# Moving the q/k transposes to the front of the SyncE queue and two v projections ahead of the last q and k, in a fused attention and gated-MLP kernel

## The chip, the cores and the metric

The kernel runs on one core of one Trainium2 chip. The metric is the device time of one execution in microseconds (us); lower is better. The core has five engines with instruction streams of their own: TensorE (PE, matrix products), ScalarE (ACT), VectorE (DVE), GpSimd (POOL) and SyncE (SP). SP here does nothing but issue DMA transfers, in the order in which they are written. Matrix products land in PSUM, which the program treats as eight banks of 512 fp32 columns; ACT and DVE empty the banks into on-chip memory.

## What is computed

The input `x` is 2048 rows of 576 columns, bf16. After a layer norm, two branches read it, and their product is added to `x`:

```python
def _A_ref(x, wqkv, wo):
    H = 32; Dh = D // H; W = 256                       # Dh = 18
    q, k, v = ...                                      # x @ wqkv, split in heads
    scores = einsum("bhqd,bhkd->bhqk", q, k) * Dh ** -0.5
    # causal, and only the last 256 keys
    p = softmax(where(mask, scores, -1e9))
    return einsum("bhqk,bhkd->bhqd", p, v) @ wo

def _B_ref(x, w_gate, w_up, w_down):                   # F = 4608
    return (sigmoid(x @ w_gate) * (x @ w_up)) @ w_down

xn = layernorm(A_x)
out = A_x + _A_ref(xn, ...) * silu(_B_ref(xn, ...))
```

## The kernel before

**Chunks and stages.** The rows are worked through in four chunks of 512 (`NCH`), each made of four blocks of 128 rows. For one chunk the stages on PE are: the q, k and v projections (line 521, twelve of them: q, k and v of each block), the gate and up products of the MLP (line 898), in which the attention scores (line 688) and the products with v (line 745) are mixed in, and the down projection `f2` (line 1045), which is made for two blocks at a time: first pair (blocks 0 and 1), second pair (blocks 2 and 3). The output projection `wo` (line 815) and the next chunk's twelve q/k/v projections stand between the first and the second pair. This change of chunks, which occurs three times, is the place that this study is about. In PE's order it reads: first pair of f2, `wo` of blocks 0 and 2, six projections, `wo` of blocks 1 and 3, six projections, second pair of f2, gate and up products of the next chunk.

**The path of q and k.** A projection writes a pair of PSUM banks. For q a DVE instruction, for k an ACT instruction (both line 579) empties it into a slot of the ring `pk`. A DMA transpose (`qkt`, line 603) then brings the slot into `qkp`, with channels on the partitions. The ring has three slots, taken in the order q0, k0, q1, k1, q2, k2, q3, k3: so k1 can be emptied only when the transpose of q0 has landed, q2 after that of k0, k2 after q1, q3 after k1, k3 after q2. A v projection (line 617) is emptied by two ACT and two DVE instructions (line 625) straight into its place `vau`; it waits for no transpose. From the keys in `qkp`, DVE makes masked copies `kd` (line 672) for each group of four heads, which the scores read.

**Banks.** f2's second pair needs the pairs of banks (0,1) and (2,3) (`F2B`). `QKV_BANKS` says in which banks the last projections may go.

**The other transfers in this place.** `wx` (`load_x`, line 847) loads two small pieces of the gate and up weights (32 KB each, tile `sat`), the first of which (gate) the gate/up stage of the next chunk uses in two early steps, whose place `XP` sets; the second (up) is used at the end of that stage. `out` (`final_cols`, line 1141) stores a finished block of 128 rows from the ring `xf`, of two slots, and `xf` (`load_xf`) loads the rows of x for a later block into the same ring: the loads for blocks 2 and 3 need the slots of blocks 0 and 1, and so wait for those stores to have landed. The twelve weight pieces of the next chunk's first three gate/up groups (`load9`, tile `wgs`, line 405) wait for the first steps of f2's second pair (`W_GATE`).

**How the order is made.** The program lists operations with dependences and plans them with a list scheduler (`schedule`, line 1145), which writes one fixed instruction order per engine; the chip then runs each engine's list in order and waits by semaphores. `deps` become waits on the chip; `odeps` only order the plan. Among the operations that an engine could take, the scheduler takes the one with the smallest start plus 40 ns times `prio` (`PRIO_NS`). A DMA counts as done in the plan at its landing, and what is ordered behind it becomes free a slack later:

```python
                free[e] = st + o.occ
                bs = max(free[e] + DMA_LAT_NS, bw)
                bw = bs + o.nbytes / DMA_BYTES_PER_NS
                o.done = bw
...
                elif o.lane is not None:
                    t = o.done + o.slack
```

These constants decide an order; they are not measured times.

Of the kernel before, what the change touches and what calls it, by code (L numbers as in the profile page):

```python
# [59 lines left out]
AVOID_NS = 20000.0  # L60
RBN = 4
XS = (13, 1, 1, 1)
XP = (4, 0)
RUN = 3
WX_PRIO = -1
WX_FT = 7
WD_AT = (14, 18, 22, 28, 29, 30, 31, 32, 33)
QKV_FIRST = "q0 q1 v0 v1 q2 v2 k0 v3 k1 q3 k2 k3"
QKV_NEXT = "q0 k0 q1 v0 v1 k1 q2 k2 v2 q3 k3 v3"
QKV_GATE = 2  # L70
QKV_PRIO = -2
QKV_CHAIN = 1
QKV_WO = {"v1": (0,), "q2": (1,)}
WO_QKV = {"k0": (1,)}
QKV_BANKS = {"q3": ((0, 1), (2, 3)), "k3": ((4, 5), (6, 7)), "v3": ((4, 5), (6, 7))}
QKV_F2 = (1, 8)
LAST = 448
W_GATE = 2
# [138 lines left out]
class Builder:  # L217
# [98 lines left out]
    def build(self):  # L316
        self.r_xr = Ring(NXR)
        self.r_xnr = Ring(NXNR)
        self.r_xn = Ring(1)
        self.r_w = Ring(RW)  # L320
        self.r_t = Ring(RT)
        self.r_pk = Ring(RPK)
        self.r_exp = Ring(NEXP)
        self.r_s = Ring(RS)
        self.r_xf = Ring(RXF)
        self.r_kd = Ring(RKD)
        self.r_rec = Ring(RREC)
        self.r_bn = Ring(RBN)
        self.op_f1 = {}
        self.build_init()  # L330
        self.op_pv = [[None] * NHG for _ in range(NCH)]
        self.op_sc = [[[] for _ in range(NHG)] for _ in range(NCH)]
        self.op_on = [[None] * NHG for _ in range(NCH)]
        self.op_mul = [[None] * NHG for _ in range(NCH)]
        self.all_kd = {}
        self.op_oc = [[[], []] for _ in range(NCH)]
        self.op_v = [None] * NQB
        self.op_tail = [None] * NHG
        self.op_hT = {}
        self.f2_last = None  # L340
        for c in range(NCH):
            self.build_ln(c)
            if c == 0:
                self.build_weights()
                self.build_wd()
            self.build_qkv(c)
            self.last_mul = None
            self.build_attn(c)
            self.load_x(c)
            self.op_pkz = [self.op("POOL", 2000, lambda e: e.memset(self.pk[:, 1:RPK, :, :], 0.0), f"pkz:{c}",  # L350
                                   deps=self.op_on[c], prio=1)]
            if c == 0:
                self.op_wo = []
            self.build_wo(c)
            self.build_ffn(c)
            if c == 0:
                self.build_late_weights()
                for o in self.ops:
                    if o.name in ("wo:0:00", "wo:0:10"):
                        o.add_dep(self.op_wo)  # L360
                for k, o in enumerate(self.op_wo):
                    self.f2_ops[(1, k % 5)].add_dep(o)
# [178 lines left out]
            "p t (h d) -> p t h d", d=DH)  # L541

    def build_qkv(self, c):
        self.op_q, self.op_k, self.op_qkt, self.op_qe = [], [], [], []
        old = [o for l in self.op_sc[c - 1] for o in l] + self.op_tail if c > 0 else []
        order = QKV_FIRST if c == 0 else QKV_NEXT
        prev = None
        for w in order.split():
            i, j = int(w[1]), "qkv".index(w[0])
            o = (self.build_v if j == 2 else self.build_qk)(c, i, j, old)  # L550
            if c > 0:
                o.odeps += [self.op_wop[x] for x in QKV_WO.get(w, ())]
                o.odeps += ([prev] if prev and QKV_CHAIN else []) + (self.op_xn[QKV_GATE] if not prev else []) + ([self.f2_ops[QKV_F2]] if QKV_F2 else [])
                o.prio = QKV_PRIO
                for x in WO_QKV.get(w, ()):
                    self.op_wof[x].odeps.append(o)
                for ps in o.alloc:
                    ps.cands = QKV_BANKS.get(w, ps.cands)
            prev = o

    def build_qk(self, c, i, j, old):
        if c == 0:
            both = self.pk[:, 0:2, :, :].rearrange("p j h d -> p (j h d)") if i == 0 else \
                self.expr[:, 2 * i - 2:2 * i, :, :].rearrange("p a b c -> p (a b c)")
            pk = both.rearrange("p (g q r s d) -> p q s g r d", g=NHG, q=2, r=2, s=2)[:, j, :, :, :, 0:DH]
            dpk = []
        else:
            spk, dpk = self.r_pk.take()
            full = self.pk[:, spk, :, :]
            pk = full[:, :, 0:DH].rearrange("p (h s) d -> p s h d", s=2)  # L570
        o, ps = self.project(c, i, j, f"qk:{c}:{i}:{j}", [], self.op_pv[c - 1][NHG - 1] if c > 0 else None)

        deps = [o, self.op_pkz] + dpk + (self.op_ez[i - 1:i] if c == 0 and i > 0 else []) + (self.op_on[c - 1] if c > 0 else [])

        def f_ev(e, part, act):
            src, dst = self.halves(ps)[:, part], pk[:, part]
            if c == 0:
                dst, src = dst[:, 0], src[:, 0].rearrange("p (g r) d -> p g r d", r=2)
            return e.activation(dst, src, ACTF.Copy) if act else e.tensor_copy(dst, src)  # L579
        ev = []  # L580
        for k, (part, act) in enumerate(((slice(0, 1), 1), (slice(1, 2), 0)) if c == 0 else ((slice(0, 2), j),)):
            n = D // 2 if c == 0 else D
            ev.append(self.rd("ACT" if act else "DVE", act_ns(n) if act else dve_ns(n),
                              lambda e, part=part, act=act: f_ev(e, part, act), f"qke:{c}:{i}:{j}:{k}", deps=deps, prio=1,
                              psum=[ps]))
        if c == 0:
            if j == 0:
                self.op_qe.append(ev)
                return o
            dst = self.qkp[:, :, :].rearrange("p g (j c) -> p (g j) c", j=2)[:, :, i * P:(i + 1) * P]  # L590
            dm = self.dma(dst, both, 2 * XT0_BYTES * 8 * P * P * 2, f"qkt:{c}:{i}", ("qk", i), deps=ev + self.op_qe[i] + old,
                          prio=0, issue=XT0_ISSUE_NS, transpose=True, slack=XT0_SLACK)
            if i > 0:
                for k in (2 * i - 2, 2 * i - 1):
                    self.r_exp.release(k, dm)
            else:
                for k in (0, 1):
                    self.r_pk.rel[k].append(dm)
            self.op_q.append(dm)
            self.op_k.append(dm)  # L600
        else:
            c0 = j * KO + i * P
            dm = self.dma(self.qkp[:, :, c0:c0 + P], full.rearrange("p h d -> p (h d)"), XT_BYTES * 8 * P * P * 2,
                          f"qkt:{c}:{i}:{j}", ("qk", i, j), deps=ev + old, prio=0, issue=XT_ISSUE_NS, transpose=True)
            self.r_pk.release(spk, dm)
            (self.op_q, self.op_k)[j].append(dm)
        self.op_qkt.append(dm)
        return o
# [47 lines left out]
    def build_kd(self, c, hg):  # L656
        self.slots_kd, self.ops_kd = {}, {}
        for g in range(1 if c == 0 else 0, 3):
# [4 lines left out]
            for half in range(2):  # L663
                def f_kd(e, g=g, s_=s_, half=half):
                    if g == 0:
                        src = self.qkp[:, hg, :].rearrange("p (j c) -> p j c", j=2)[:, :, CH:CH + P].rearrange(
                            "p j (b c) -> p j b c", b=2)
                        dst = self.kd[:, s_, :, half, :].rearrange("p (j b) c -> p j b c", j=2)
                    else:
                        src = self.qkp[:, hg, KO + (g - 1) * 256:KO + g * 256].rearrange("p (b c) -> p b c", b=4)  # L670
                        dst = self.kd[:, s_, :, half, :]
                    return e.tensor_scalar(dst, src, self.hm[:, half:half + 1], None, ALU.mult)  # L672
                self.ops_kd[g].append(self.op("DVE", KD_NS, f_kd, f"kd:{c}:{hg}:{g}{half}", deps=deps, prio=KD_PRIO))
        self.all_kd[hg] = [o for l in self.ops_kd.values() for o in l]

    def build_unit(self, c, hg, u, pieces, masks):
# [170 lines left out]
    def load_x(self, c):  # L847
# [4 lines left out]
        for n, (w, f, j, r0) in enumerate(src):  # L852
            a = w[:, f:f + P].rearrange("(j p) c -> p j c", p=64)[:, j:j + 3:2, :]
            dst = self.sat[r0:r0 + 64, self.sx, 0:2 * P].rearrange("p (j c) -> p j c", j=2)
            self.op_wx.append(self.dma(dst, a, 2 * W_FACTOR * 64 * 2 * P * 2, f"wx{n}:{c}", ("wx", n), deps=dx, prio=WX_PRIO))
            self.r_s.release(self.sx, self.op_wx[-1])

    def build_ffn(self, c):
# [257 lines left out]
    def build_final(self, sb, ps, o_f2, sth, dth, ss, o_s):  # L1116
# [2 lines left out]
        self.r_s.release(ss, q2)  # L1119
        self.r_exp.release(sth, q3)  # L1120
        self.r_xf.release(sx, o_o)

    def final_cols(self, sb, ps, o_f2, sth, dth, ss, o_s, sx, o_x, c0, c1):
        op = self.op
# [285 lines left out]
```

## Time and profile before

| | |
|---|---|
| median of three runs | 559.36 us (559.29, 559.36, 560.3) |
| the profiled execution | 559.26 us, of which the profile's span is 557.5 us and 1.76 us lies around it |
| PE busy | 552.2 us, 99% of the span; granted clock 1.00 |
| DVE, ACT, POOL busy | 312.2, 279.4, 29.2 us |
| DMA | 73.35 MB, mean 132 GB/s |
| the three changes of chunks (first projection to the first f2 step of the second pair) | from 122.27, 259.56 and 397.69 us to 137.71, 275.83 and 413.13 us |

In the lines of the profile a row reads: start, duration, engine, source line, operation, output <- input, shapes, count; a bracket at the end is the engine's idle time just before and what ended it. SPq is SP's issuing of a DMA; "to landing" is the time from the issue to the data's arrival.

### The profile page before, as it was taken

To read this page: it belongs to the slowest core of one execution; us is meant where nothing else is said; L and a number is where in the kernel's file an instruction comes from. 1 tells how busy PE (TensorE), PEld (TensorE's weight loads), DVE (VectorE), ACT (ScalarE), POOL (GpSimd) and SP (SyncE) were. 2 spreads that over 40 slices of the span, in tenths; PEclk is the share of its full clock that TensorE was granted. 3 is DMA by queue.
4 is the path that set the end of the run, shared out by engine and by line. 5 is a ranking of instruction groups with operands and counts; after the bars stand their busy time and mean duration, and the time that the engine had idled before them with its cause. 6 is when DMAs were issued, how large, how long until landed. Compare 5 with 4: busy or idle time off the path is not lost.

```text
span 557.5 us, 18764 instructions
## 1 busy us (share of the span) xinstructions
PE 552.2 (99%) x8144; PEld 310.2 (56%) x8146; DVE 312.2 (56%) x906; ACT 279.4 (50%) x395; POOL 29.2 (5%) x58
## 2 busy tenths in 40 slices
PE   8999999999999999999999999999999999999998
PEld 5755555567555455556655554545665554554554
DVE  5436998425067988633407798843430785885111
ACT  7436886124076767602307778740330875873031
POOL 3000110100000100010000011001000000000100
PEclk9999999999999999999999999999999999999999
DMA  8999868938945666235993666422399355651001
GB/s 201 221 203 209 210 183 215 241 62 152 205 106 132 141 155 138 56 52 66 167 214 89 150 142 148 104 63 65 63 169 203 86 130 130 139 130 34 21 25 41
DMA packets 125929, 73.35 MB, mean 132 GB/s; under 512 B 54680, under 2 KB 125336, under 8 KB 125848
## 3 DMA queue, kind: packets, MB, share of 16 engines
q1 hardware_dynamic: 125848, 72.16, 61.5%
q8 instruction: 64, 1.05, 0.8%
q14 instruction: 17, 0.14, 0.1%
HBM read 55.48 MB, written 2.36 MB: 104 GB/s over the span
## 4 chain that ended last, share of the span: by engine, by line
PE 96%; DMA 2%; ACT 1%; DVE 1%; issue 0%; ACTq 0%; SPq 0%
PE ps L898 50%; PE ps L1045 22%; PE ps L521 7%; PE ps L688 6%; PE ps L745 4%; PE ps L815 3%; DMA qkp<-pk 2%; PE ps L1100 2%; PE ps L1076 2%; PE ps L396 1%; ACT xn L507 0%; DVE pk L579 0%; DVE expr L1135 0%; ACT expr L1133 0%; ACT sat L840 0%
## 5 line engine op out<-in xcount | busy, mean ns | idle before, releaser
L898 PE MATMUL ps<-xn,wgs 64*128 64x512 bf16 x2522 | 299.3, 376 | 0.0
L898 PEld LDWEIGHTS ps<-xn,wgs 64*128 64x128 bf16 x2522 | 121.5, 94 | 114.1 <-issue 1.4
L703 ACT ACTIVATE expr<-ps 128x1024 bf16<-128x1024 f32 (+1 forms) x152 | 150.7, 1019 | 23.9 <-PE ps L688 23.8
L916 DVE SCALAR_TENSOR_TENSOR hT<-tring,ps 128x512 bf16<-128x512 bf16 x144 | 98.2, 682 | 54.8 <-PE ps L898 35.0
L912 ACT ACTIVATE tring<-ps 128x512 bf16<-128x512 f32 x144 | 86.4, 600 | 82.3 <-PE ps L898 61.8
L1045 PE MATMUL ps<-wd_sb,hT 64*128 64x512 bf16 (+1 forms) x2016 | 125.5, 283 | 0.7 <-DVE pk L579 0.7
L1045 PEld LDWEIGHTS ps<-wd_sb,hT 64*128 64x128 bf16 x2016 | 65.8, 94 | 59.4 <-issue 1.0
L717 DVE TENSOR_TENSOR expr<-expr,m 128x256 bf16<-128x256 bf16 (+1 forms) x272 | 61.3, 267 | 6.4 <-ACT expr L703 5.9
L688 PE MATMUL ps<-qkp,kd 64*128 64x320 bf16 (+4 forms) x720 | 56.7, 252 | 0.0
L521 PE MATMUL ps<-wqkv_sb,xn 64*128 64x288 bf16 x864 | 54.4, 283 | 0.1
L688 PEld LDWEIGHTS ps<-qkp,kd 64*128 64x128 bf16 x720 | 34.2, 94 | 33.3 <-issue 0.8
L672 DVE TENSOR_SCALAR kd<-qkp,hm 128x256 bf16<-128x256 bf16 x176 | 40.5, 290 | 16.6 <-DMA qkp<-pk 14.3
L1133 ACT ACTIVATE expr<-ps 128x576 bf16<-128x576 f32 (+2 forms) x17 | 9.8, 620 | 76.8 <-PE ps L1045 61.4
L521 PEld LDWEIGHTS ps<-wqkv_sb,xn 64*128 64x128 bf16 x864 | 43.0, 94 | 9.4 <-ACT xn L507 0.2
L1135 DVE SCALAR_TENSOR_TENSOR expr<-expr,ps 128x576 bf16<-128x576 bf16 x12 | 8.5, 751 | 63.8 <-ACT expr L1133 63.8
L840 ACT ACTIVATE sat<-ps 128x576 bf16<-128x576 f32 x16 | 9.5, 648 | 64.8 <-PE ps L815 64.8
L1137 DVE TENSOR_TENSOR expr<-expr,sat 128x576 bf16<-128x576 bf16 (+2 forms) x17 | 7.2, 437 | 43.7 <-ACT expr L1133 34.4
L761 DVE STREAM_TRANSPOSE pk<-ps 128x512 f32<-128x512 f32 x32 | 21.4, 697 | 17.2 <-PE ps L745 17.2
L727 POOL COPY qkp<-qkp 128x256 bf16<-128x256 bf16 x24 | 10.2, 425 | 264.4 <-DVE kd L672 264.4
L778 DVE STREAM_TRANSPOSE op__63<-pk 128x512 bf16<-128x512 bf16 x32 | 22.3, 701 | 0.1
L745 PEld LDWEIGHTS ps<-expr,vau 64*32 64x32 bf16 x1440 | 18.1, 92 | 7.4 <-issue 5.5
L745 PE MATMUL ps<-expr,vau 64*32 64x320 bf16 (+4 forms) x1440 | 20.8, 254 | 0.0
(55 smaller groups left out, 223.0 us busy)
## 6 DMA issues: line engine op xcount, KB each, us to landing
wgs<-in_B_w_gate_dram SPq DMA_DIRECT2D x47, 240.0 KB, 3.8
wgs<-in_B_w_up_dram SPq DMA_DIRECT2D x47, 240.0 KB, 4.8
wgs<-in_B_w_up_dram SPq DMA_DIRECT2D x47, 192.0 KB, 4.2
wgs<-in_B_w_gate_dram SPq DMA_DIRECT2D x47, 192.0 KB, 4.6
wd_sb<-in_B_w_down_dram SPq DMA_DIRECT2D x9, 576.0 KB, 6.9
xf<-in_A_x_dram SPq DMA_DIRECT2D x18, 144.0 KB, 2.5
out_dram<-xf SPq DMA_DIRECT2D x15, 144.0 KB, 2.1
xr<-in_A_x_dram SPq DMA_DIRECT2D x14, 144.0 KB, 4.2
```

The lines of the kernel that those rows point to most:

```text
L521: r = e.matmul(self.bank(ps, HV, hf), self.xn[r0:r0 + 64, k, i * P:(i + 1) * P], self.wqkv_sb[r0:r0 + 64, j, k, :], start=(k == 0), stop=( ...
L672: return e.tensor_scalar(dst, src, self.hm[:, half:half + 1], None, ALU.mult)
L688: i = e.matmul(self.bank(ps, 512, r)[:, pos * 64:(pos + n) * 64], w, self.qkp[r0:r0 + 64, hg, q0 * 64:(q0 + n) * 64], start=True, stop=Tru ...
L703: return e.activation(self.expr[:, es, :, 0:ncol], src, ACTF.Exp, scale=SM_SCALE)
L717: return e.tensor_tensor(ap, ap, m, ALU.mult)
L745: r = e.matmul(self.bank(ps2[s_])[32 * cg:32 * cg + 32, q0 * 64:(q0 + n) * 64], vf[:, v0:v0 + 32], self.expr[p0:p0 + 64, es, cg % 2, pos * ...
L761: tr = self.rd("DVE", dve_ns(CH), lambda e, tf=tf, s_=s_: e.transpose(tf, self.bank(ps2[s_])), f"t1:{c}:{t}", deps=[o, self.op_mul[c][t - ...
L778: t2 = self.op("DVE", dve_ns(CH), lambda e, on=on: e.transpose(self.op_[:, hg % NOT, :], on.rearrange("p g d -> p (g d)")), f"t2:{c}:{hg}" ...
L898: return e.matmul(self.bank((pg, pu)[gu][ft]), w, self.xn[r0:r0 + 64, i, :], start=first, stop=last, tile_position=(r0, 0))
L912: return e.activation(self.tring[:, st_, :], self.bank(ps), ACTF.Tanh, scale=0.5)
L916: return e.scalar_tensor_tensor(self.hT[:, ft, :], self.tring[:, st_, :], 1.0, self.bank(ps), ALU.add, ALU.mult)
L1045: r = e.matmul(self.ps[:, b + n0:b + n1], self.hT[r0:r0 + 64, ft, i * P:(i + 1) * P], self.wd_sb[r0:r0 + 64, q, ft % WDG, n0:n1], start=(s ...
```

## The change

Six edits, all of them on the chunks after the first except the first one, which holds for every chunk:

1. `XP`: the two steps that use the small gate piece stand at step 5 and 6 of the stretch, not 4 and 5.
2. The q/k transposes get the priority -4 (was 0) in the plan of SP.
3. The stores of blocks 0 and 1 of the chunk before, and both small weight pieces, are ordered behind all eight transposes, with priority -3 (`odeps`, so the plan only; no wait is added on the chip).
4. The order of the projections ends "v2 v3 q3 k3" (was "v2 q3 k3 v3").
5. `QKV_BANKS`: v2 and v3 go into banks (0,1) or (2,3), q3 and k3 into (4,5) or (6,7) (before: q3 in the first two, k3 and v3 in the others, v2 free).
6. The first head group's `kd` copies are ordered behind the emptying of every q and k and of the last v.

```diff
-XP = (4, 0)
+XP = (5, 0)
+HELD_PRIO = -3
+QKT_PRIO = -4
-QKV_NEXT = "q0 k0 q1 v0 v1 k1 q2 k2 v2 q3 k3 v3"
+QKV_NEXT = "q0 k0 q1 v0 v1 k1 q2 k2 v2 v3 q3 k3"
-QKV_BANKS = {"q3": ((0, 1), (2, 3)), "k3": ((4, 5), (6, 7)), "v3": ((4, 5), (6, 7))}
+QKV_BANKS = {"v2": ((0, 1), (2, 3)), "v3": ((0, 1), (2, 3)), "q3": ((4, 5), (6, 7)), "k3": ((4, 5), (6, 7))}
...
     def build_qkv(self, c):
...
             prev = o
+        for o in self.op_out[-QPC:-FIN]:
+            o.odeps += self.op_qkt
+            o.prio = HELD_PRIO
+        self.op_out = []
...
+        self.op_ev += ev
...
-                          f"qkt:{c}:{i}:{j}", ("qk", i, j), deps=ev + old, prio=0, issue=XT_ISSUE_NS, transpose=True)
+                          f"qkt:{c}:{i}:{j}", ("qk", i, j), deps=ev + old, prio=QKT_PRIO, issue=XT_ISSUE_NS, transpose=True)
...
-                self.ops_kd[g].append(self.op("DVE", KD_NS, f_kd, f"kd:{c}:{hg}:{g}{half}", deps=deps, prio=KD_PRIO))
+                self.ops_kd[g].append(self.op("DVE", KD_NS, f_kd, f"kd:{c}:{hg}:{g}{half}", deps=deps, prio=KD_PRIO,
+                                              odeps=self.op_v[c * QPC + QPC - 1] + self.op_ev if c > 0 and hg == 0 else []))
...
     def load_x(self, c):
...
+            if c > 0:
+                self.op_wx[-1].odeps += self.op_qkt
+                self.op_wx[-1].prio = HELD_PRIO
...
     def build_final(...):
+        self.op_out.append(o_o)
```

More of the change, by code (lines that the diff above doesn't have):

```diff
@@ L543, in build_qkv @@
     def build_qkv(self, c):
-        self.op_q, self.op_k, self.op_qkt, self.op_qe = [], [], [], []
+        self.op_q, self.op_k, self.op_qkt, self.op_qe, self.op_ev = [], [], [], [], []
         old = [o for l in self.op_sc[c - 1] for o in l] + self.op_tail if c > 0 else []
@@ L559, in build_qkv @@
             prev = o
+        for o in self.op_out[-QPC:-FIN]:
+            o.odeps += self.op_qkt
+            o.prio = HELD_PRIO
+        self.op_out = []
     def build_qk(self, c, i, j, old):
```

## The prediction

> **What bounds the kernel now.** I read the page first, then the list of what PE waited for, then PE's order of time at the three changes of chunks.
>
> ```profile
> span 557.5 us, 18764 instructions
> PE 552.2 (99%) x8144; PEld 310.2 (56%) x8146; DVE 312.2 (56%) x906; ACT 279.4 (50%) x395; POOL 29.2 (5%) x58
> ```
>
> ```profile
> PE ps L396 <- DVE hm L381: 1.5, 1, 1.5
> PE ps L1045 <- DVE pk L579: 0.7, 1, 0.7
> ```
>
> PE is busy 552.2 of 557.5 us, so all that any edit of waiting could return is 5.3 us, and of the waits (in total, times, longest) only one lies at a change of chunks: the second pair of f2 (line 1045) waited for DVE's emptying of a projection into `pk` (line 579). The 1.5 us is the start of the program, which the change does not reach. The same stretch of six projections shows what that wait costs, because it occurs three times:
>
> ```profile
> 131.09 6.78 PE L521 MATMUL ps<-wqkv_sb,xn 64*128 64x288 bf16 x108
> 137.71 3.54 PE L1045 MATMUL ps<-wd_sb,hT 64*128 64x512 bf16 x52
> ...
> 268.38 6.78 PE L521 MATMUL ps<-wqkv_sb,xn 64*128 64x288 bf16 x108
> 275.83 6.49 PE L1045 MATMUL ps<-wd_sb,hT 64*128 64x512 bf16 x100 [0.67 <-DVE pk L579]
> ...
> 406.51 6.78 PE L521 MATMUL ps<-wqkv_sb,xn 64*128 64x288 bf16 x108
> 413.13 5.06 PE L1045 MATMUL ps<-wd_sb,hT 64*128 64x512 bf16 x79
> ```
>
> From start to start it is 6.62 us in the first and third change of chunks (137.71 - 131.09, 413.13 - 406.51) and 7.45 us in the second (275.83 - 268.38). So the stall is worth 0.83 us, not the bracket's 0.67: the bracket begins at the modelled end of the last product, which overlaps what follows. This is the only gap that the edits aim at. Why it arose stands in the chain of waits:
>
> ```profile
> 262.62 5.48 DMA qkp<-pk
> ...
> 268.18 0.65 ACT pk L579
> ...
> 269.69 4.69 DMA qkp<-pk
> ...
> 274.41 0.48 DVE kd L672 x2
> ...
> 274.93 0.77 DVE pk L579
> ```
>
> The reader follows the ring: q0's transpose, issued at 262.62, lands 5.48 us later; only then may ACT empty k1 (268.18); k1's transpose, issued at 269.69, lands at 274.38; only then may q3 be emptied, and DVE has two `kd` copies (0.48 us) in front of it. q3 lies in a bank that f2's second pair needs, so PE stands until 275.7.
>
> **The change part by part.**
>
> *Order of the projections, and banks (edits 4 and 5).* No product is added or removed. Six projections in 6.62 us are 1.10 each, so from 268.38 the new order ends q2 at 269.48, k2 at 270.59, v2 at 271.69, v3 at 272.79, q3 at 273.90, k3 at 275.00, and f2 could start at 275.00. It now needs the banks of v2 and v3, which wait for no transpose.
>
> ```profile
> 269.89 0.76 DVE L579 CAST pk<-ps 128x576 bf16<-128x576 f32 x1
> ...
> 271.89 0.95 DVE L625 CAST vau<-ps 64x288 bf16<-64x288 f32 x2 [0.88 <-PE ps L521]
> ```
>
> ```profile
> 268.72 1.19 ACT L840 ACTIVATE sat<-ps 128x576 bf16<-128x576 f32 x2
> 270.89 0.66 ACT L579 ACTIVATE pk<-ps 128x576 bf16<-128x576 f32 x1 [0.98 <-DMA qkp<-pk]
> 271.89 0.84 ACT L625 ACTIVATE vau<-ps 64x288 bf16<-64x288 f32 x2 [0.34 <-PE ps L521]
> ```
>
> v2 was emptied from 271.89, 0.20 us behind its product, in 0.95 us on DVE and 0.84 on ACT. v3, one projection later, is thus emptied from 272.99 to 273.94: 1.06 us ahead of f2's start. What stands in front of it on the in-order engines? On ACT k1, the two `wo` emptyings, k2 and v2. Even if q0's transpose is again as late as 5.48 us, k1 goes at 268.18, the `wo` pair to 269.91, k2 from 270.79 to 271.45, v2 at 271.89: nothing moves. On DVE q2 (0.76 us, at the latest 270.65 as in the row) and v2. The banks that the last six take are free in time as well: q2's by 270.65 against v3's start at 271.69, the `wo` pair's by 269.91 against v2 at 270.59 and q3 at 272.79, k2's by 271.55 at the latest against k3 at 273.90. The wait goes, and nothing is next: the margin is about a microsecond. Worth: -0.83 us, once.
>
> q3 and k3 are emptied about when they were, in banks that are next taken by the gate/up stage, behind the whole second pair of f2. Cost 0.
>
> *First keys behind the emptying (edit 6).* The four `kd` copies move behind q3 on DVE. Behind them waits the first score product only:
>
> ```profile
> 293.47 1.24 PE L898 MATMUL ps<-xn,wgs 64*128 64x512 bf16 x9
> 294.35 0.38 PE L898 MATMUL ps<-xn,sat 64*128 64x512 bf16 x1
> ...
> 295.41 0.40 PE L688 MATMUL ps<-qkp,kd 64*128 64x320 bf16 x4
> ```
>
> That is at 295.41, some 20 us after k3's projection; two copies take 0.48. Cost 0. The gain of 0.48 us that it would have made by itself is inside the 0.83.
>
> *Transposes first (edits 2 and 3).* SP's queue in this stretch:
>
> ```profile
> 262.62 1.24 SPq L256 DMA_TRANSPOSE qkp<-pk  x1
> 263.89 1.66 SPq L257 DMA_DIRECT2D sat<-in_B_w_gate_dram  x1
> 265.61 0.66 SPq L257 DMA_DIRECT2D sat<-in_B_w_up_dram  x1
> 266.31 2.71 SPq L256 DMA_TRANSPOSE qkp<-pk  x2
> 269.06 0.58 SPq L257 DMA_DIRECT2D out_dram<-xf  x1
> 269.69 4.83 SPq L256 DMA_TRANSPOSE qkp<-pk  x3
> 274.57 0.58 SPq L257 DMA_DIRECT2D out_dram<-xf  x1
> 275.20 0.43 SPq L257 DMA_DIRECT2D xf<-in_A_x_dram  x1
> 275.71 2.59 SPq L256 DMA_TRANSPOSE qkp<-pk  x2
> 278.34 0.63 SPq L257 DMA_DIRECT2D wgs<-in_B_w_gate_dram  x1
> ...
> 287.26 0.66 SPq L257 DMA_DIRECT2D xf<-in_A_x_dram  x1
> ```
>
> Between the transposes stand two small pieces (2.42 us from 263.89), two stores and a load of x (1.6). All leave, so k0's and q1's transposes go out some 2.4 us sooner, and the last one when k3 is emptied: 275.00 + 0.20 + 0.65, so at about 275.9 instead of 277.0, done at 277.2. PE gains nothing more from that, since the stall is gone already. The weight pieces start at 277.2 instead of 278.34. Where do the held four go? In the plan they come free when the last transpose has landed, 1.6 + 0.98 us behind its issue, plus 0.6 of slack: 3.2 us, in which five pieces of 0.66 are planned. So: five pieces, two stores, two small pieces, seven pieces, two loads of x. Twelve pieces took 8.92 us (278.34 to 287.26), 0.74 each: the stores go at 280.9, the small pieces at 282.1 and 282.8. How long do they take to land? Nearest rows, the last lines of the views by tile, `sat`, `wgs`, `xf` and `qkp` in turn:
>
> ```profile
> DMA to landing us min/median/max: 3.1/3.8/4.4
> ```
>
> ```profile
> DMA to landing us min/median/max: 4.0/6.8/7.6
> ```
>
> ```profile
> DMA to landing us min/median/max: 1.7/2.1/7.1
> ```
>
> A small piece alone took up to 4.4 us, the pieces in the crowd up to 7.6. I take the crowd's, since they now stand in it: the gate piece is there by 289.7. PE needs it at 294.35 - 0.83, plus one step by edit 1 (the up piece only at the end of the stage). A step is two products side by side:
>
> ```profile
> 293.65 1.94 PE ps L898 x18
> ```
>
> that is 1.94 / 9 = 0.22 us, so at 293.7: 4.0 us of cover. Cost 0; with the cover gone, what is lost stands under the second rival. The pieces behind the held four are those of groups two and three, first needed 5.8 and 11.7 us into the stage (three tiles of 1.94 each), at 298 at the earliest; the last is issued at 287.9 and landed by 295.5. The loads of x follow at 288.6 and 289.3, landed by 295.7 and 296.4 at 7.1 us. The additions that need them:
>
> ```profile
> 297.04 0.45 DVE L1139 TENSOR_TENSOR xf<-xf,expr 128x576 bf16<-128x576 bf16 x1
> ...
> 297.75 0.45 DVE L1139 TENSOR_TENSOR xf<-xf,expr 128x576 bf16<-128x576 bf16 x1
> ```
>
> 0.83 sooner these stand at 296.2 and 296.9: half a microsecond of room even at the slowest landing, and the plan, which counts a slack of 5 us behind these loads, will set them later. I take 0.
>
> *Edit 1* moves two steps by one place: 0 us, with 0.22 us more time for the piece. Two steps instead of three then stand between the two halves of that accumulation; the bound is one step, 0.22 us a chunk, if PE had to wait there. It is a loss only; I take 0, for the range up to 0.9 over four chunks.
>
> **Sum.** 559.26 - 0.83 = 558.43 us for the profiled execution; the span would be 556.7, with the same 1.76 around it. The median of the runs is 0.10 above the profiled one. I predict 558.4.
>
> **Rivals.**
>
> *The wait changes its name.* f2 would wait for v3 instead, or k2's emptying would hold PE at k3, if transposes sent back to back landed much later than those spaced by other transfers. Against it: v3 waits for no transpose, and ACT's k2 has 1.4 us of room. For it: the landing of 5.48 us in the row above is unexplained, and one that is later by over a microsecond in the second change of chunks would bring back most of the 0.83. Time: 559.3. The same number would come out if the planner, with other priorities, wrote an order that does not do what the diff says.
>
> *Held small pieces come too late (slower).* If the planner puts the held four behind all twelve weight pieces, the stores go at 277.2 + 8.92 = 286.1 and the gate piece at 287.3. PE asks for it at 293.7. At the 4.4 us of the `sat` row it lands at 291.7 and there is no stall; at the 7.1 of the `xf` row, which belongs to a load issued in just that place, at 294.4, and PE stands for 0.7 us; at the 7.6 of the `wgs` row for 1.2. The point from which it decides is a landing of 6.4 us; halfway between the last two, 0.95 us in each of three changes of chunks, gives 558.43 + 2.85 = 561.3. Against it: by the constants of the plan they follow the fifth piece. The Trainium skill, "DMA: Bandwidth & Descriptors", section "Queues, rings and completion order", speaks for this rival: on each DMA engine the descriptors of one queue are taken in ring order, so a small transfer cannot overtake the large ones ahead of it. The trace agrees so far: a load of x behind the twelve pieces took 7.1 us where the least in that view is 1.7.
>
> **How the numbers follow.** The runs shown spread over 0.18%, so about 0.2%, 1.12 us, is what a measurement here can tell from no change: faster means below 558.24, slower above 560.48. Forecast 0.71, at 557.9 to 558.9; its middle, 558.4, is only 0.2 us from the bound, so 0.26 of it falls below and 0.45 inside. Wait renamed 0.14, all inside. Pieces too late 0.15, slower. That makes 0.26, 0.59 and 0.15. The range runs from the forecast's lower end to the first rival with some of edit 1's bound: 557.9 to 559.8.
>
> **What would show it.** Right: PE's list of waits has no line 1045 behind line 579; the six projections to f2 take 6.62 us in all three changes; eight transposes stand together in SP's queue; `kd` follows the last line 579. Wrong: a wait of line 898 for `sat` (second rival), or of line 1045 for line 625 (first); a DVE wait at line 1139 for `xf`, passed on to PE; or a new gap at a place that the edits do not name.

## The result, and the profile after

The changed kernel takes 558.57 us (median of 20 runs, 558.02 to 558.62) against 559.33 us before (20 runs, 558.37 to 560.81). The ratio on record is 0.9984, with a 95% interval from 0.9977 to 0.9991 (the quotient of the two medians is 0.9986). The prediction was 558.4 us, and a gain of 0.83 on the profiled execution; the profiled executions took 559.26 and 558.37 us, 0.89 apart, with spans of 557.5 and 556.6.

In the changed kernel line 1045 of before (f2) is line 1057, 521 (projections) is 524, 579 (emptying into `pk`) is 586, 625 (emptying of v) is 633, 672 (`kd`) is 680, 898 (gate and up) is 910. First the page, and the whole list of what PE waited for:

```profile
span 556.6 us, 18762 instructions
...
PE 551.4 (99%) x8144; PEld 307.7 (55%) x8146; DVE 313.7 (56%) x906; ACT 279.8 (50%) x395; POOL 31.6 (6%) x58
```

```profile
PE ps L399 <- DVE hm L384: 1.5, 1, 1.5
PE ps L498 <- DVE xnr L472: 0.6, 1, 0.6
PE ps L524 <- ACT xn L510: 0.3, 1, 0.3
PE ps L1088 <- issue: 0.2, 1, 0.2
```

No wait of f2 is left; what is listed belongs to the first chunk and the last blocks. PE's order of time at the three changes of chunks:

```profile
130.99 6.78 PE L524 MATMUL ps<-wqkv_sb,xn 64*128 64x288 bf16 x108
137.61 4.73 PE L1057 MATMUL ps<-wd_sb,hT 64*128 64x512 bf16 x70
...
268.28 6.78 PE L524 MATMUL ps<-wqkv_sb,xn 64*128 64x288 bf16 x108
274.90 8.42 PE L1057 MATMUL ps<-wd_sb,hT 64*128 64x512 bf16 x118
...
405.60 6.78 PE L524 MATMUL ps<-wqkv_sb,xn 64*128 64x288 bf16 x108
412.21 5.96 PE L1057 MATMUL ps<-wd_sb,hT 64*128 64x512 bf16 x90
```

All three stretches now take 6.62 us (the third 6.61); the second took 7.45. The other 0.1 us of the span was already gained at 130.99 (131.09 before) and is followed up with edit 1 below. DVE in the second change of chunks:

```profile
272.89 0.95 DVE L633 CAST vau<-ps 64x288 bf16<-64x288 f32 x2 [0.15 <-PE ps L524]
274.07 0.76 DVE L586 CAST pk<-ps 128x576 bf16<-128x576 f32 x1 [0.22 <-PE ps L524]
274.74 0.87 DVE L680 TENSOR_SCALAR kd<-qkp,hm 128x256 bf16<-128x256 bf16 x4
```

v3 is emptied at 273.84, 1.06 us ahead of f2, q3 behind it, and the copies of the keys last. SP's queue, then the landing of the two small pieces (from their view by tile), then PE's use of the first:

```profile
262.52 14.96 SPq L258 DMA_TRANSPOSE qkp<-pk  x8
277.52 0.71 SPq L259 DMA_DIRECT2D wgs<-in_B_w_gate_dram  x1
...
280.95 1.88 SPq L259 DMA_DIRECT2D out_dram<-xf  x2
282.88 0.61 SPq L259 DMA_DIRECT2D sat<-in_B_w_gate_dram  x1
...
288.80 1.87 SPq L259 DMA_DIRECT2D xf<-in_A_x_dram  x2
```

```profile
DMA to landing us min/median/max: 4.1/4.3/4.5
```

```profile
293.62 0.38 PE L910 MATMUL ps<-xn,sat 64*128 64x512 bf16 x1
```

Eight transposes stand in one row, then five weight pieces, the two stores, and the small pieces from 282.88. The gate piece landed at 287.4 (4.5 us after its issue), and PE used it at 293.62, some 6 us later.

### The profile page after: what moved, and what is told of

It is laid out like the page before. It is cut to its first block, busy times and chain, and to the rows that moved or that the text cites. A ratio compares the mean times of both kernels' runs of the same rounds, so it can differ in the third digit from the quotient of the medians.

```text
span 556.6 us, 18762 instructions
## 1 busy us (share of the span) xinstructions
PE 551.4 (99%) x8144; PEld 307.7 (55%) x8146; DVE 313.7 (56%) x906; ACT 279.8 (50%) x395; POOL 31.6 (6%) x58
## 3 DMA queue, kind: packets, MB, share of 16 engines
q8 instruction: 64, 1.05, 0.8%
## 4 chain that ended last, share of the span: by engine, by line
PE 98%; DMA 0%; DVE 0%; ACT 0%; issue 0%; SPq 0%
PE ps L910 50%; PE ps L1057 22%; PE ps L524 10%; PE ps L697 6%; PE ps L754 4%; PE ps L824 3%; PE ps L1112 2%; PE ps L1088 2%; DMA xr<-in_A_x_dram 0%; ACT xn L510 0%; PE ps L498 0%; SPq L259 0%; DVE bnst L461 0%; DVE xnr L472 0%; DVE mv L465 0%
## 5 line engine op out<-in xcount | busy, mean ns | idle before, releaser
L1057 PEld LDWEIGHTS ps<-wd_sb,hT 64*128 64x128 bf16 x2016 | 64.6, 94 | 59.7
L736 POOL COPY qkp<-qkp 128x256 bf16<-128x256 bf16 x24 | 12.3, 512 | 261.2 <-DVE kd L680 261.2
```

The lines of the kernel that those rows point to most:

```text
L1057: r = e.matmul(self.ps[:, b + n0:b + n1], self.hT[r0:r0 + 64, ft, i * P:(i + 1) * P], self.wd_sb[r0:r0 + 64, q, ft % WDG, n0:n1], start=(s ...
```

## The experiments

Eleven kernels were run, in three groups; each group has its own runs of the kernel before, on the same chip: 559.78 us for the first four, 559.44 for the next four, 559.66 for the last three. Every comparison is within its group.

### Edits 4 and 5 alone

```diff
-QKV_NEXT = "q0 k0 q1 v0 v1 k1 q2 k2 v2 q3 k3 v3"
+QKV_NEXT = "q0 k0 q1 v0 v1 k1 q2 k2 v2 v3 q3 k3"
...
-QKV_BANKS = {"q3": ((0, 1), (2, 3)), "k3": ((4, 5), (6, 7)), "v3": ((4, 5), (6, 7))}
+QKV_BANKS = {"v2": ((0, 1), (2, 3)), "v3": ((0, 1), (2, 3)), "q3": ((4, 5), (6, 7)), "k3": ((4, 5), (6, 7))}
```

> Edits 4 and 5 alone (order v2 v3 q3 k3 and the new banks) on the kernel before. If order and banks carry the gain by themselves, as the prediction has it: no wait of f2 in any change of chunks, 558.5 us. If f2 is only free of the transposes when nothing that waits for one stands ahead of v3's emptying on DVE: two kd copies are still planned between v2's and v3's emptying, so v3 is emptied behind k1's landing; in an execution like the profiled one f2 starts at about 275.9 instead of 275.8, now behind line 625, and the time stays at 559.3. If earlier transposes carry the gain: 559.3 too, since they are where they were. A side effect to watch: k3's transpose, now last, is planned behind the twelve weight pieces; the third score product needs it, which is planned 22 us behind f2's start, so no loss is expected.

Measured: 560.83 us, ratio 1.0022 (1.0008 to 1.0037): slower. The runs spread from 560.04 to 563.95, and the profiled one took 562.31, well above the median, so its waits need not be the usual ones. PE's waits there:

```profile
PE ps L688 <- DVE expr L1135: 1.6, 3, 0.7
...
PE ps L1045 <- DVE vau L625: 1.2, 1, 1.2
```

The second row is what the second theory expected: f2 now waits for the emptying of v, because DVE has the copies of the keys ahead of it, and these wait for a transpose:

```profile
275.88 0.48 DVE L672 TENSOR_SCALAR kd<-qkp,hm 128x256 bf16<-128x256 bf16 x2 [1.90 <-DMA qkp<-pk]
276.39 0.95 DVE L625 CAST vau<-ps 64x288 bf16<-64x288 f32 x2
```

The first row, a wait of the scores in each change of chunks, was foreseen by no theory; the expectation had called its cause harmless. It is shown by the next kernel.

### Edits 4, 5 and 6

The kernel above, with the first keys ordered behind the emptying:

```diff
-                self.ops_kd[g].append(self.op("DVE", KD_NS, f_kd, f"kd:{c}:{hg}:{g}{half}", deps=deps, prio=KD_PRIO))
+                self.ops_kd[g].append(self.op("DVE", KD_NS, f_kd, f"kd:{c}:{hg}:{g}{half}", deps=deps, prio=KD_PRIO,
+                                              odeps=self.op_v[c * QPC + QPC - 1] + self.op_ev if c > 0 and hg == 0 else []))
```

> Edits 4, 5 and 6 together (order, banks, keys behind the emptying), the queue of SP planned with the priorities of the kernel before. If f2 is free once nothing that waits for a transpose stands ahead of v2's and v3's emptying: 558.5 and no wait of f2, wherever the transposes land (k3's is planned behind the twelve weight pieces here too). If earlier transposes carry the gain: 559.3.

Measured: 560.33 us, ratio 1.0011 (1.0002 to 1.002): still slower. f2 waits for nothing, so the decoupling works. But the scores (line 694 here) wait in two of the three changes of chunks, 0.45 us in the first and 0.75 in the second:

```profile
296.47 0.39 PE L694 MATMUL ps<-qkp,kd 64*128 64x320 bf16 x4 [0.75 <-DVE expr L1142]
```

SP and DVE tell why, with the transpose's landing in the last row:

```profile
285.49 4.45 SPq L258 DMA_TRANSPOSE qkp<-pk  x1
```

```profile
295.17 0.48 DVE L677 TENSOR_SCALAR kd<-qkp,hm 128x256 bf16<-128x256 bf16 x2 [18.49 <-DMA qkp<-pk]
295.57 1.41 DVE L1142 SCALAR_TENSOR_TENSOR expr<-expr,ps 128x576 bf16<-128x576 bf16 x2
```

```profile
DMA to landing us min/median/max: 9.6/9.6/9.6
```

With k3 as the last projection, its transpose becomes ready together with the weight pieces, and at its old priority it is planned behind all twelve. Issued at 285.49 (SP alone needed 4.45 us for it), it landed 9.6 us later. The copies of the last keys wait for it on DVE; behind them in DVE's order stand the two instructions that read f2's results out of its banks (line 1142), and the first scores need one of these banks. The room of 22 us that the expectation counted to the third score product was real; what it missed is who is queued behind the waiting copy.

### The transposes' priority with it

Edits 2, 4, 5 and 6: the kernel above with

```diff
-QKT_PRIO = 0
+QKT_PRIO = -4
```

> Edits 2, 4, 5 and 6: as the kernel with edits 4, 5 and 6 together, but the transposes have the priority -4; stores and small pieces are not held. If what made that kernel slow was k3's transpose behind the twelve weight pieces: k3's transpose now goes out ahead of them, the scores wait for nothing, and the time is that of the changed kernel, 558.6. If the stores and small pieces between the transposes matter by themselves: up to 0.8 us of wait comes back, 559.3.

Measured: 558.71 us, ratio 0.9981 (0.9972 to 0.999), against 558.53 us, 0.9983 (0.9974 to 0.9991), for the changed kernel run again beside it, whose own expectation was:

> The changed kernel once more, as the yardstick for the three beside it: every theory says 0.8 to 1.0 us under the kernel before on the same chip, no wait of f2, and no wait of the scores for DVE.

Both hold. PE waits for neither f2's banks nor the scores' in either. So what made edits 4, 5 and 6 slow was k3's transpose behind the weight pieces, and the same wait of the scores was in edits 4 and 5 alone; f2's own wait there went with edit 6. Holding the stores and small pieces is not needed for the gain. The 0.18 us between the two has the size of edit 1 (below).

This kernel also shows what order and banks do, once the copies are out of the way. Here k1's transpose goes out at 270.17, as late against the projections as in the kernel before, and DVE still waits for it:

```profile
275.20 0.76 DVE L583 CAST pk<-ps 128x576 bf16<-128x576 f32 x1 [1.02 <-DMA qkp<-pk]
```

```profile
275.23 17.80 PE L1051 MATMUL ps<-wd_sb,hT 64*128 64x512 bf16 x288
```

q3 is emptied 0.73 us after f2 has started (275.96 against 275.23), and f2 does not wait for it. That is the prediction's mechanism.

### Edit 6 alone

> Edit 6 alone (first keys behind the emptying) on the kernel before. If the kd copies ahead of q3 on DVE were the whole cause: 558.5. If the landing of k1's transpose is the root and the copies only add to it: q3 is emptied from its landing (274.4 in the trace of before) to 275.2, and f2 starts 0.2 to 0.35 late instead of 0.83: 558.7 to 558.9. If neither matters without earlier transposes: 559.3.

Measured: 559.11 us, ratio 0.9989 (0.9978 to 1.0). In its profile f2 (line 1051) still waits; the lines are from PE's and from DVE's order of time:

```profile
268.73 6.78 PE L524 MATMUL ps<-wqkv_sb,xn 64*128 64x288 bf16 x108
275.71 4.53 PE L1051 MATMUL ps<-wd_sb,hT 64*128 64x512 bf16 x68 [0.20 <-DVE pk L583]
```

```profile
274.81 0.76 DVE L583 CAST pk<-ps 128x576 bf16<-128x576 f32 x1 [1.62 <-DMA qkp<-pk]
```

q3's emptying still waits for the transpose of k1, now without two copies ahead of it. From start to start it is 6.98 us, so 0.36 us of the stall is left, and 0.47 is gone. The landing is the root and the copies add to it, as the second theory had it, though the time is 0.2 us over its window. The medians differ by 0.67 us in its group, but with that interval they cannot tell 0.47 from nothing.

### Edits 2 and 3 alone

> Edits 2 and 3 alone (transposes first on SP, stores and small pieces behind) on the kernel before. If earlier transposes carry the gain: k1's transpose goes out at about 268.4 instead of 269.7 and lands by 272.3 to 273.5, the copies and q3 are done by 274.8 at the latest, f2 waits for nothing: 558.5. If only the decoupling by order and banks, or the copies' place, carries it: 559.3.

Measured: 558.74 us, ratio 0.998 (0.9971 to 0.9989), with runs from 558.47 to 558.79: nearly the whole gain, with the old order, the old banks, and the keys ahead of q3.

```profile
273.20 0.48 DVE L680 TENSOR_SCALAR kd<-qkp,hm 128x256 bf16<-128x256 bf16 x2
273.72 0.76 DVE L586 CAST pk<-ps 128x576 bf16<-128x576 f32 x1
```

The copies no longer wait, and q3 is emptied by 274.48. Counted from the first of these six projections, its emptying begins some 0.3 us later than in the profile of edits 1, 2, 3 and 6 (below), where no copy stands ahead of it, but in time for f2, which waits for nothing here.

### Edits 1, 2 and 3; edits 1, 2, 3 and 6; and the changed kernel without edit 1

> Edits 1, 2 and 3 alone: transposes first and step 5, with the old order, banks and place of the keys. If these three hold the whole gain: 558.55, the changed kernel's time, with its narrow spread. If edits 4 to 6 add something: 558.7 or more.

> The changed kernel without edits 4 and 5: transposes first, keys behind the emptying, step 5, but the old order and the old banks. If early transposes are enough: q3 is emptied by 273.8 and f2 waits for nothing, 558.55 as the changed kernel. If order and banks are needed for the last part: a wait of f2 for line 579's successor in some executions, 558.7 to 559 and a wider spread of the runs.

> The changed kernel without edit 1 (step 4 as before). The kernels with step 4 show a gap of 0.14 us on PE at 45.6 us, just behind the step with the small piece in the first chunk; the two profiles with step 5 do not. If edit 1 removes that gap: it is back here, 558.67 to 558.7. If it is chance: 558.55.

Measured: 558.55 us, ratio 0.9981 (0.9972 to 0.9989), for edits 1, 2 and 3 alone; 558.56, 0.9981 (0.9973 to 0.999), with edit 6 as well; 558.76, 0.9983 (0.9974 to 0.9992), for the changed kernel without edit 1. Edits 1 to 3 hold the whole gain; 4, 5 and 6 add nothing that can be measured on top, and no kernel run here is measurably faster than the changed one.

Edit 1 was set at 0 and is worth about 0.2 us in the medians: 558.76 without it against 558.56 and 558.55 with it in this group, 558.71 against 558.53 in the one above. (These kernels differ in one or more other edits too, which made no difference that could be measured.) In the first chunk PE stood shortly ahead (the expectation said behind) of the step with the small piece. PE's order of time, the kernel before and then the changed one:

```profile
44.66 1.39 PE L898 MATMUL ps<-xn,wgs 64*128 64x512 bf16 x9
45.68 0.39 PE L898 MATMUL ps<-xn,sat 64*128 64x512 bf16 x1
```

```profile
44.76 1.46 PE L910 MATMUL ps<-xn,wgs 64*128 64x512 bf16 x11
45.85 0.38 PE L910 MATMUL ps<-xn,sat 64*128 64x512 bf16 x1
```

Of the products ahead of the small piece's own, one is its partner in the same step; the others are two to a step of 0.216 us. In the changed kernel that makes five steps, 1.08 us, and the small piece comes 1.09 us behind the first. In the kernel before it makes four steps, 0.86 us, and the small piece comes 1.02 us behind: 0.14 of it is a gap (the halves of a step lie 0.02 apart). In the later chunks of the kernel before the same stretch has no gap (0.88 us from 293.47). The gap is in all seven profiled kernels that have the old step, the one without edit 1 among them, and in none of the six profiles with the new one. What ends it is not shown, as the trace names no releaser, and neither is where the rest of the 0.2 us comes from. In two of the eleven runs without edit 1, 559.78 and 559.93 us, another wait came on top (in the profiled one, `wo` for the transfer into `oT`, 0.7 us); its cause was not studied.

### The second rival: the held transfers behind all weight pieces

```diff
-HELD_PRIO = -3
+HELD_PRIO = 3
```

> The changed kernel with the held stores and small pieces behind all twelve weight pieces (priority +3 instead of -3). The prediction's second rival: the gate piece goes out at about 287.3 and PE asks for it at 293.7; with a landing of 7.1 to 7.6 us PE stands 0.7 to 1.2 us in each change of chunks, 560.5 to 562.0. With the 4.1 to 4.5 us that the two small pieces took in the changed kernel: landed by 292, no wait, the time of the changed kernel.

Measured: 561.36 us, ratio 1.0032 (1.0021 to 1.0044). From the waits, from SP's and PE's order of time and from the view by tile:

```profile
PE ps L910 <- DMA sat<-in_B_w_gate_dram: 2.2, 3, 0.9
```

```profile
288.22 0.61 SPq L259 DMA_DIRECT2D sat<-in_B_w_gate_dram  x1
```

```profile
295.33 0.37 PE L910 MATMUL ps<-xn,wgs 64*128 64x512 bf16 x1 [0.65 <-DMA sat<-in_B_w_gate_dram]
```

```profile
DMA to landing us min/median/max: 6.5/6.7/7.0
```

This is the prediction's second rival as it was priced (561.3): three waits, of up to 0.9 us, with a landing of up to 7.0 us behind twelve pieces, where five pieces ahead gave 4.5. In both kernels the gate piece lands about 0.2 us behind the second of the two stores issued just ahead of it (287.37 behind 287.13 in the changed kernel, 295.19 behind 295.02 here), and in none of the thirteen profiles does a transfer of SP's queue land ahead of one issued before it. The Trainium skill's rule that each DMA engine takes the descriptors of one queue in ring order ("DMA: Bandwidth & Descriptors", section "Queues, rings and completion order") is borne out by these landings.

### The banks exchanged

```diff
-QKV_BANKS = {"v2": ((0, 1), (2, 3)), "v3": ((0, 1), (2, 3)), "q3": ((4, 5), (6, 7)), "k3": ((4, 5), (6, 7))}
+QKV_BANKS = {"v2": ((4, 5), (6, 7)), "v3": ((4, 5), (6, 7)), "q3": ((0, 1), (2, 3)), "k3": ((0, 1), (2, 3))}
```

> The changed kernel with the banks exchanged: q3 and k3 in those that f2's second pair needs, v2 and v3 in the others. f2 then waits for k3's emptying on ACT (275.16 to 275.82 in the changed kernel, where f2 starts at 274.90): about 0.97 us in each of the three changes of chunks, 2.9 us in all, 561.5. If the banks did not matter once the transposes are early: 558.6.

Measured: 561.79 us, ratio 1.0039 (1.0026 to 1.0051), and one row of waits for all three changes of chunks:

```profile
PE ps L1057 <- ACT pk L586: 3.0, 3, 1.2
```

So the new order needs the new banks: k3, now the last projection, is emptied only after f2 could have started, so it must not stand in f2's banks. The yardstick kernel's 558.53 us and this row's 3.0 add up to 561.5.

## Why the prediction was right, and where its steps were not

**The stall and its size: right.** f2's wait for line 579, priced from start to start at 0.83 us instead of by the bracket's 0.67, went; 7.45 us became 6.62. The medians of the runs lie 0.76 us apart. That this is so close is in part luck: about 0.2 of it belongs to edit 1, which was put at nothing, and the one execution profiled before happened to show a stall close to the difference of the medians. The range, 557.9 to 559.8, was wide enough to hold no change at all (559.33); it is the interval of the ratio, and the experiments, that show the gain.

**Which edit brings it: wrong.** The prediction put the whole -0.83 on edits 4 and 5, and said of the transposes' place that "PE gains nothing more from that". Alone, edits 4 and 5 cost 1.05 us (560.83 against 559.78); edits 2 and 3 alone gain 1.04 (558.74). There are two ways to free f2, earlier transposes (edits 2 and 3) or banks that wait for none (edits 4, 5 and 6), and each suffices for f2; the second was a gain only with edit 2 beside it (558.71 against 559.44), and a loss without it (560.33 against 559.78). In the changed kernel both are at work at once: there q3's emptying no longer waits for a transpose. The step that failed is the one on edits 4 and 5: it looked at ACT and DVE with edit 6 already in place, and not at what the new order does to the queue of SP, where k3's transpose falls behind twelve weight pieces unless edit 2 holds it in front.

**Keys behind the emptying, cost 0: right**; its own gain was put at 0.48; its profile shows 0.47, its median 0.67 (559.11 against 559.78), with an interval that reaches to no gain.

**Held transfers, cover of 4.0 us: right in sign.** The cover was 6.2 us (293.62 less 287.4). The landing was mis-sized: 7.6 us was taken from the weight pieces, 4.5 was the most that the small pieces took. The order, behind the fifth piece, was as worked out from the plan's constants, and the additions that need `xf` waited for nothing.

**Edit 1, 0 us: wrong by about 0.2**, with the sign that the prediction excluded ("a loss only").

**First rival (the wait changes its name): did not occur in the changed kernel.** Edits 4 and 5 alone show a wait of that name, f2 behind line 625, 1.2 us, but for another reason: the copies of the keys ahead on DVE, not transposes sent back to back. **Second rival: did not occur**, and would have had the predicted price.

**The late landing of q0's transpose** (5.48 us) was not caused by the small pieces behind it. With eight transposes in a row and nothing between, ACT in the second change of chunks still waits for it:

```profile
267.72 0.65 ACT L586 ACTIVATE pk<-ps 128x576 bf16<-128x576 f32 x1 [1.70 <-DMA qkp<-pk]
```

It landed 5.1 us after its issue at 262.52. The traces show what goes with it. The profile lists a separate queue, `q8 instruction`, with one transfer of 16 KB every 4 to 13 us (from 60 us on). In the second change of chunks of the kernel before, such a transfer started at 263.77, while q0's transpose was under way, and another at 272.30, while k1's was (4.69 us); none fell on k0's and q1's (3.36 and 3.20). The row of that queue (transfers, MB, share of the DMA time) from the issue of q0's transpose to its landing, and then the same for k1's:

```profile
q8 instruction: 1, 0.02, 1.6%
```

```profile
q8 instruction: 1, 0.02, 1.5%
```

Over all thirteen profiles, the first chunk and the six transposes behind twelve weight pieces left out, 168 transposes of q and k met no such transfer between 0.5 us before their issue and their landing, and landed after at most 3.8 us; the 138 that met one took 4.4 us in the median and up to 5.7. So the stall came with two such meetings in one change of chunks, one on the way to k1's emptying and one on its transpose; in the first change, of these four, only q1's and k1's met one (3.23 and 4.37 us), in the third only k0's and q1's (4.62 and 4.24), and f2 did not wait. Whether the transfer on `q8` is itself what delays the others, or only comes with it, is not shown.

## What to carry to other kernels

Price a stall from start to start against an equal stretch without it, and ask which of several edits could each remove it: a sum over parts that are not independent says nothing about the parts. When an operation moves to a later place, look for what else becomes ready at that moment in every queue that its followers use, and for what stands behind a waiting instruction on its engine: here a DVE copy that was not needed for microseconds held up the freeing of PSUM banks. When a wait depends on DMA landings, removing it may show more in the spread of the runs than in the median. When a landing is late for no reason in its own queue, look at the other DMA queues in the same stretch.

## What the runs showed of the hardware that was not expected

The spread: the 20 runs before range over 2.44 us and reach down to the changed kernel's times, those of the changed kernel range over 0.60. The profiled execution had the removed wait in one change of chunks of three. That it differs from execution to execution as well is what the spread suggests; only one execution before was profiled, and that its 0.83 us lies close to the median's gain is luck of the draw.

A DMA transpose issued behind twelve weight pieces held SP for 4.45 us and landed after 9.6 us (the six such transposes in the two kernels that have them took 8.1 to 9.6); without a crowd ahead the eight transposes of the same change of chunks landed after 3.2 to 5.5 us, as the view of `qkp` in the kernel before has it (the fourth of the views that the prediction names):

```profile
DMA to landing us min/median/max: 3.2/3.8/5.5
```
